# Attention planner: a table of parameters with finer rows, and the instruction orders that follow

## The chip, the cores and the metric

The kernel runs on one core of a Trainium2 chip. The metric is the device time of one execution in microseconds; lower is better. Five engines work from instruction queues of their own: PE (matrix multiply), ACT (activation functions), DVE (vector work), POOL (general elementwise work) and SP (which issues most DMAs).

## The reference

Two attention blocks over 2048 tokens of width 512, with 32 heads of 16, their outputs side by side:

```python
# A: linear attention
phi = lambda t: jnp.where(t > 0, t + 1, jnp.exp(t)) + 1e-6
pq, pk = phi(q), phi(k)
kv = jnp.einsum("bhsd,bhse->bhde", pk, v)
z = jnp.einsum("bhsd->bhd", pk)
num = jnp.einsum("bhqd,bhde->bhqe", pq, kv)
den = jnp.einsum("bhqd,bhd->bhq", pq, z)[..., None] + 1e-6
# B: softmax attention
scores = jnp.einsum("bhqd,bhkd->bhqk", q, k) * scale
p = _softmax(scores, axis=-1)
o = jnp.einsum("bhqk,bhkd->bhqd", p, v)
# both: q, k, v = x @ wqkv before, @ wo after; then
return jnp.concatenate([a, b], axis=-1)
```

The work is in B: 32 heads x 2048 x 2048 scores, each of which needs an exponential.

## The kernel before

**Work units.** B is cut into 32 units (NU): four groups of eight heads, four chunks of 512 queries, and two sets of four heads (even and odd). A unit has 64 score blocks (UB): 16 key tiles times four heads, each block 128 keys x 512 queries. So there are 2048 blocks. The four heads of a unit lie in the four row groups of PE's array, so up to four blocks are made at the same time.

**Two ways through a block.** PE makes the scores into a PSUM bank (`qk`, line 907). Then either

- ACT takes the exponential of two or three neighbouring banks in one instruction (`fill_act_cand`, line 1056; the instruction is line 1129), into as many slots of the shared buffer MEM. The planner calls the third block "more" (line 1082), and A3 in the table allows it. Banks 0, 1 and 4, 5 are ACT's pairs (SLOT); the third block takes bank 2 or 3 (OPT).
- or DVE computes an approximate exponential with integer arithmetic on the bits of an fp16 number (line 1008, one bank or two neighbouring ones), and POOL makes two shifted copies of the result (line 1204), so that this block fills three slots and is multiplied with three weighted versions of V. DVE's banks are 6, 3 and 2 (DSET).

PE then multiplies each slot with V into one PSUM bank (line 1259): one product for a block of ACT, three for a block of DVE. When a unit's products are complete, DVE transposes and normalizes them (lines 1289 to 1303).

**The rest of the work** is cut into jobs: projections of B (`proj_job`, `v4_job`; the matmuls in column tiles are line 644, the evacuations lines 681 to 751), the linear branch A (its exponentials are L768 on ACT, its other steps L769 to L829 on DVE), output projections (line 648 copies their results) and stores. They share PE, DVE and DVE's banks with B.

**The order.** The instruction order of each engine is found while the program is built, by a list planner (the loop from line 1527 on). It keeps a model clock T for each engine, collects what each could start next (`fill_act_cand`: scores for ACT; `fill_d_cand`: scores for DVE; `pv_cand`: products with V; `job_cand`: projections and the like), and takes the earliest, with priorities for ties. Thus nobody decides beforehand how many blocks go to DVE: it is what the order leaves. `fill_in` (line 1495) puts dummy matmuls (line 1518) into planned gaps of PE. Planned durations are in the code, for one exponential of ACT `d = 0.04 + w * 0.000845` us for w columns (line 1125), and for a change between PE's row, column and other tilings SW = 0.1 us.

**The table.** Thirteen parameters of the planner come from a table row, chosen by the model clock of PE:

```python
WAITN, WAITM, DLOW, DLOW2, PVO, PVQ, PVR, JPR, DLEAD, DBL, RES, LIM, A3 = TABLE[min(int(T["pe"] / TSEG), len(TABLE) - 1)]
```

- WAITN, WAITM, DLOW: when DVE's planned backlog is under DLOW, the next scores for ACT may be put off until WAITN of DVE's banks are free, so that scores for DVE go along with them.
- DLOW2: the backlog under which a third block for ACT is refused when DVE could have one. A3: whether a third block is allowed at all.
- PVO, PVQ, PVR: when a batch of products with V is taken, and how many rounds it may have.
- JPR: the priority of a job's matmuls. DLEAD, DBL: how early scores for DVE are made, and how large DVE's backlog may grow.
- RES: buffer slots kept in reserve. LIM: how close to ACT running dry other PE work may come.

The head of the program, up to the first exponential, is a hand-written order that the table doesn't touch. DMAs of the jobs are issued by SP in the order of the plan.

Of the kernel before, what the change touches and what calls it, by code (L numbers as in the profile page):

```python
# [259 lines left out]
def bass_concat_heads__linear_attn_block__softmax_full_mha__prompt_kernel(nc, A_x, A_wqkv, A_wo, B_x, B_wqkv, B_wo, out):  # L260
# [34 lines left out]
    TSEG = 5  # L295
    TABLE = [
        (2, 0.2, 0.3, 1, 8, 13.5, 2, 0.8, -0.5, 4, 6, 0.1, 1),
        (2, 0, 2, 0.6, 5, 10, 2, 0.8, 0.2, 4, 6, 0.15, 1),
        (2, 0, 2, 0.6, 5, 10, 2, 0.8, 0.2, 4, 6, 0.15, 1),
        (2, 0, 2, 0.6, 12, 11, 2, 0.8, 0.2, 4, 6, 0.15, 1),  # L300
        (2, 0, 1, 0.6, 12, 11, 2, 0.8, 0.5, 4, 6, 0.15, 1),
        (2, 0, 1, 0.6, 12, 11, 2, 0.8, 0.5, 2, 6, 0.15, 0),
        (2, 0, 1, 0.6, 12, 13.5, 2, 0.8, 0.5, 2, 8, 0.15, 0),
        (2, 0.1, 2, 0, 5, 12.5, 2, 2, -0.5, 3, 8, 0.15, 0),
        (1, 0.1, 0.6, 0, 5, 12.5, 2, 2, -0.5, 4, 8, 0.15, 0),
        (2, 0.1, 0.6, 0.6, 5, 12.5, 2, 2, -0.5, 4, 8, 0.15, 0),
        (2, 0, 1.5, 0.6, 12, 13.5, 2, 2, -0.5, 3, 8, 0.15, 0),
        (2, 0, 1.5, 0.6, 12, 13.5, 2, 0.8, -0.5, 3, 6, 0.15, 0),
        (1, 0, 1.5, 0.6, 5, 13.5, 2, 0.8, -0.5, 3, 4, 0.15, 0),
        (1, 0.1, 1.5, 0.6, 3, 13.5, 2, 2, -0.5, 3, 8, 0.15, 0),  # L310
        (1, 0, 0.6, 1, 16, 10, 2, 2, 0.5, 3, 4, 0.15, 0),
        (1, 0, 1, 1, 16, 8, 2, 2, 0.2, 3, 8, 0.15, 1),
        (1, 0, 1, 1, 3, 8, 2, 2, 0.2, 3, 6, 0.15, 1),
        (1, 0, 1, 0.3, 3, 8, 2, 0.8, 0.2, 3, 6, 0.1, 1),
        (3, 0, 2, 0.3, 3, 8, 2, 2, 0.2, 3, 6, 0.1, 1),
        (3, 0, 2, 0.3, 3, 8, 2, 2, 0.2, 2, 4, 0.15, 1),
        (3, 0, 2, 0.3, 16, 8, 2, 2, 0.2, 3, 4, 0.15, 1),
        (1, 0, 1.5, 0.3, 3, 11, 3, 2, -0.5, 2, 6, 0.06, 1),
        (1, 0, 1.5, 0.3, 3, 11, 2, 2, -0.5, 2, 6, 0.06, 1),
        (1, 0.1, 2, 0.3, 3, 11, 2, 2, 0, 2, 4, 0.15, 1),  # L320
        (1, 0, 2, 0.3, 3, 11, 2, 2, 0, 4, 4, 0.06, 1),
        (1, 0, 2, 0.3, 3, 12.5, 2, 2, 0, 4, 4, 0.1, 1),
        (1, 0, 2, 0.3, 3, 8, 3, 2, 0.5, 4, 4, 0.1, 1),
        (1, 0.2, 2, 0.3, 3, 8, 3, 2, 0.5, 2, 6, 0.1, 1),
        (1, 0.2, 2, 0.3, 3, 8, 3, 2, 0.5, 2, 6, 0.1, 1),
        (3, 0, 2, 0.3, 3, 8, 3, 2, 0.5, 2, 6, 0.1, 1),
        (2, 0.3, 1.5, 0, 16, 13.5, 2, 2, -0.5, 3, 6, 0.1, 1),
        (3, 0.3, 1.5, 0, 12, 13.5, 2, 2, 0.2, 3, 6, 0.1, 1),
        (2, 0.3, 1.5, 0.3, 3, 10, 2, 2, 0.2, 3, 6, 0.1, 1),
        (3, 0.3, 1.5, 0.3, 12, 13.5, 2, 0.8, 0.2, 3, 8, 0.1, 1),  # L330
        (3, 0.3, 1.5, 0.3, 12, 13.5, 2, 0.8, 0.2, 3, 8, 0.1, 1),
        (3, 0.05, 2, 0, 12, 13.5, 2, 0.8, 0, 3, 4, 0.1, 1),
        (3, 0.2, 1, 0, 5, 13.5, 2, 0.8, 0.8, 3, 6, 0.06, 1),
        (1, 0.1, 1.5, 0.6, 8, 13.5, 2, 0.8, 0.5, 4, 4, 0.06, 1),
        (3, 0.1, 1.5, 0.6, 8, 13.5, 2, 0.8, 0.5, 4, 4, 0.06, 1),
        (1, 0, 1, 0, 8, 8, 2, 2, -0.5, 4, 4, 0.15, 1),
        (1, 0, 1, 0, 8, 8, 2, 2, -0.5, 4, 4, 0.15, 1),
        (1, 0.1, 1, 1, 8, 12.5, 2, 2, -0.5, 2, 6, 0.15, 1),
        (1, 0.3, 2, 1, 8, 11, 2, 0.8, 0, 2, 6, 0.02, 0),
        (2, 0.05, 0.6, 0.3, 16, 8, 3, 0.8, 0.8, 4, 4, 0.06, 0),  # L340
        (1, 0.05, 1, 0.3, 5, 8, 2, 2, 0.2, 2, 6, 0.06, 1),
        (1, 0.2, 2, 0.3, 16, 8, 3, 2, -0.5, 2, 4, 0.06, 0),
        (1, 0.3, 2, 0.6, 12, 13.5, 3, 2, -0.5, 2, 4, 0.06, 0),
        (1, 0.3, 2, 0.6, 12, 13.5, 3, 2, -0.5, 2, 4, 0.06, 1),
        (1, 0.3, 2, 1, 16, 13.5, 2, 0.8, -0.5, 2, 4, 0.06, 1),
        (1, 0.1, 0.6, 0, 5, 9, 2, 2, 0, 2, 4, 0.06, 0),
        (1, 0.1, 0.3, 0, 5, 9, 2, 0.8, -0.5, 3, 8, 0.02, 0),
        (2, 0, 0.6, 0.3, 8, 13.5, 2, 2, -0.5, 2, 4, 0.06, 0),
        (2, 0.2, 0.3, 0.6, 12, 12.5, 2, 0.8, 0, 4, 8, 0.1, 0),
        (1, 0.1, 2, 0.6, 16, 12.5, 2, 0.8, 0.2, 3, 4, 0.15, 1),  # L350
        (1, 0.05, 2, 0.6, 16, 8, 2, 0.8, 0.2, 3, 8, 0.1, 1),
        (3, 0.05, 2, 0.6, 16, 8, 2, 0.8, 0.2, 4, 8, 0.02, 1),
        (3, 0.05, 0.6, 0.6, 16, 8, 2, 0.8, 0.5, 4, 8, 0.02, 1),
        (2, 0.05, 0.6, 0.6, 16, 8, 2, 0.8, 0.2, 4, 8, 0.02, 1),
        (2, 0.2, 2, 0.6, 8, 8, 3, 0.8, 0, 3, 8, 0.15, 1),
        (1, 0.1, 1.5, 0, 12, 13.5, 2, 0.8, -0.5, 2, 6, 0.02, 1),
        (1, 0.1, 1.5, 0, 12, 13.5, 2, 0.8, -0.5, 2, 6, 0.15, 1),
        (1, 0.1, 1, 1, 12, 13.5, 2, 0.8, -0.5, 2, 4, 0.15, 1),
        (1, 0.1, 1, 0, 12, 13.5, 2, 0.8, -0.5, 2, 4, 0.15, 1),
        (1, 0.1, 0.3, 0, 12, 13.5, 2, 0.8, -0.5, 4, 6, 0.15, 0),  # L360
        (1, 0.1, 2, 1, 12, 13.5, 2, 0.8, -0.5, 2, 8, 0.15, 1),
        (1, 0.1, 2, 1, 12, 13.5, 2, 0.8, -0.5, 2, 4, 0.15, 1),
        (1, 0.1, 2, 1, 12, 13.5, 2, 0.8, -0.5, 2, 4, 0.1, 1),
        (3, 0.2, 2, 0.6, 16, 12.5, 2, 0.8, 0.8, 3, 4, 0.15, 0),
        (3, 0.2, 2, 0.6, 16, 13.5, 2, 0.8, 0.8, 3, 4, 0.15, 0),
        (3, 0.2, 0.6, 0, 5, 13.5, 2, 0.8, 0.8, 3, 4, 0.1, 0),
        (3, 0.2, 0.6, 0, 12, 10, 2, 0.8, 0.8, 2, 4, 0.1, 0),
        (3, 0.3, 1, 0.6, 3, 8, 2, 0.8, 0.8, 2, 6, 0.15, 0),
        (2, 0.3, 1.5, 0.6, 3, 10, 2, 0.8, -0.5, 3, 6, 0.15, 1),
        (3, 0, 2, 0.6, 16, 9, 2, 0.8, 0.5, 4, 4, 0.15, 0),  # L370
        (2, 0.2, 1, 0.3, 5, 10, 2, 2, 0.2, 4, 6, 0.02, 0),
        (2, 0.2, 1, 0, 5, 8, 2, 2, 0.2, 4, 6, 0.02, 0),
        (1, 0.1, 2, 1, 12, 9, 2, 0.8, 0.5, 4, 4, 0.15, 0),
        (2, 0.1, 2, 1, 12, 9, 2, 0.8, 0.5, 4, 4, 0.15, 1),
        (1, 0.2, 1, 0.6, 16, 13.5, 2, 0.8, -0.5, 4, 4, 0.15, 1),
        (3, 0.1, 1, 0.6, 16, 9, 2, 0.8, -0.5, 4, 4, 0.15, 1),
        (1, 0.05, 2, 0.6, 12, 12.5, 2, 0.8, 0.2, 2, 4, 0.15, 1),
        (3, 0.1, 1.5, 0.6, 5, 9, 2, 0.8, 0, 3, 8, 0.15, 1),
        (1, 0.1, 1.5, 1, 16, 9, 2, 0.8, 0, 2, 8, 0.15, 1),
        (1, 0.1, 1.5, 0.6, 16, 9, 2, 0.8, 0.5, 2, 8, 0.15, 1),  # L380
        (1, 0.2, 1, 0.6, 5, 12.5, 2, 2, 0.5, 3, 8, 0.15, 1),
        (1, 0.2, 0.6, 0.6, 12, 10, 2, 2, 0, 2, 4, 0.1, 1),
        (3, 0, 1.5, 1, 5, 9, 2, 0.8, -0.5, 2, 6, 0.15, 1),
        (2, 0.2, 0.3, 0.6, 3, 9, 2, 2, 0, 2, 6, 0.06, 0),
        (1, 0.1, 2, 0.6, 5, 11, 2, 0.8, 0, 4, 8, 0.1, 1),
        (1, 0, 2, 0.6, 5, 11, 2, 0.8, 0, 4, 8, 0.1, 1),
        (1, 0.2, 2, 1, 5, 11, 2, 0.8, 0, 4, 4, 0.1, 1),
        (1, 0.2, 2, 0.3, 5, 11, 2, 0.8, 0, 4, 6, 0.1, 1),
        (1, 0.2, 1, 0.6, 5, 11, 3, 0.8, 0, 4, 4, 0.1, 1),
        (3, 0.3, 0.6, 1, 3, 9, 2, 0.8, -0.5, 2, 4, 0.06, 1),  # L390
        (1, 0.3, 0.6, 1, 5, 8, 2, 0.8, 0.5, 4, 4, 0.1, 1),
        (2, 0.3, 1.5, 1, 3, 8, 2, 0.8, -0.5, 2, 8, 0.06, 1),
        (2, 0.3, 1.5, 1, 5, 10, 2, 0.8, 0.2, 3, 8, 0.15, 1),
        (2, 0.2, 0.6, 0.3, 12, 8, 2, 0.8, 0.8, 4, 4, 0.15, 0),
        (3, 0, 0.6, 0.3, 8, 9, 2, 2, 0.5, 4, 6, 0.15, 0),
        (2, 0, 1, 0.3, 8, 10, 2, 0.8, 0.5, 4, 6, 0.15, 0),
        (1, 0.1, 0.3, 1, 3, 10, 2, 0.8, -0.5, 2, 8, 0.1, 0),
        (2, 0, 1, 0.3, 8, 10, 2, 0.8, 0.5, 4, 6, 0.15, 0),
        (2, 0, 1, 0.3, 12, 10, 2, 0.8, 0.2, 2, 6, 0.15, 0),
        (2, 0.1, 1, 0.3, 5, 9, 3, 0.8, 0, 2, 4, 0.15, 0),  # L400
        (1, 0, 0.6, 0, 8, 13.5, 3, 2, 0.8, 3, 4, 0.1, 0),
        (1, 0.1, 2, 0.6, 16, 8, 2, 2, 0, 3, 8, 0.02, 1),
        (2, 0, 2, 1, 5, 9, 2, 0.8, 0.5, 3, 8, 0.02, 1),
        (3, 0.05, 2, 0.3, 5, 12.5, 2, 2, 0.2, 4, 4, 0.1, 0),
        (3, 0.05, 2, 0.3, 5, 12.5, 2, 0.8, 0.5, 4, 8, 0.02, 0),
        (1, 0.05, 0.3, 1, 8, 10, 2, 0.8, -0.5, 4, 4, 0.02, 0),
        (1, 0, 0.3, 0.3, 8, 8, 2, 2, 0.5, 4, 4, 0.06, 1),
        (1, 0, 1, 0, 16, 9, 2, 0.8, 0, 3, 6, 0.15, 1),
        (2, 0.05, 2, 0.6, 3, 13.5, 2, 0.8, 0.8, 3, 8, 0.06, 1),
        (2, 0.05, 1.5, 1, 12, 10, 2, 2, 0.5, 2, 4, 0.06, 1),  # L410
        (1, 0.05, 2, 0.3, 5, 11, 2, 2, 0.8, 2, 8, 0.15, 1),
# [1278 lines left out]
```

## Time and profile before

| what | value |
|---|---|
| median of 3 runs (lowest, highest) | 656.95 us (656.53, 657.69) |
| the profiled execution, its own time | 655.85 us |
| its span, first to last instruction | 654.1 us |
| PE busy, instructions | 640.7 us (98%), 8388 |
| weight loads of PE (PEld) | 207.3 us (32%) |
| DVE | 594.7 us (91%), 1022 |
| ACT | 640.8 us (98%), 692 |
| POOL | 420.4 us (64%), 718 |
| mean granted TensorE clock | 0.997 |
| DMA | mean 27 GB/s over the span |

A row of the profile's groups names line, engine, operation, output and input tile and shape, the number of instructions, then their busy time and the mean time of one in ns, then the idle time of that engine just ahead of them and what ended it. The busy time is a union: instructions of one engine overlap in the record, so the mean of one is more than its share. In a row of busy times by stretch, the columns are the stretch, its length with the busy time of PE, then PEld, DVE, ACT and POOL, each with its number of instructions, then granted clock, DMA share and GB/s. A row of the timeline gives the start and length of a run of equal instructions.

### The profile page before, as it was taken

To read this page: it belongs to the slowest core of one execution; us is meant where nothing else is said; L and a number is where in the kernel's file an instruction comes from. 1 tells how busy PE (TensorE), PEld (TensorE's weight loads), DVE (VectorE), ACT (ScalarE), POOL (GpSimd) and SP (SyncE) were. 2 spreads that over 40 slices of the span, in tenths; PEclk is the share of its full clock that TensorE was granted. 3 is DMA by queue.
4 is the path that set the end of the run, shared out by engine and by line. 5 is a ranking of instruction groups with operands and counts; after the bars stand their busy time and mean duration, and the time that the engine had idled before them with its cause. 6 is when DMAs were issued, how large, how long until landed. Compare 5 with 4: busy or idle time off the path is not lost.

```text
span 654.1 us, 19881 instructions
## 1 busy us (share of the span) xinstructions
PE 640.7 (98%) x8388; PEld 207.3 (32%) x8389; DVE 594.7 (91%) x1022; ACT 640.8 (98%) x692; POOL 420.4 (64%) x718
## 2 busy tenths in 40 slices
PE   9999999999999999999999999999999999999996
PEld 5322333333443333333222222223332222222221
DVE  6999999978888989898999999999899999999994
ACT  6999999999999999999999999999999999999995
POOL 6588766634557656674667767766557756667772
PEclk9999999999999999999999999999999999999998
DMA  9910000000000000000011001100010100110011
GB/s 212 252 54 2 1 2 3 11 10 11 10 3 2 3 2 3 3 9 10 10 22 45 2 2 35 26 10 14 8 30 20 26 10 33 35 42 19 17 35 38
DMA packets 35808, 17.61 MB, mean 27 GB/s; under 512 B 26496, under 2 KB 35200, under 8 KB 35712
## 3 DMA queue, kind: packets, MB, share of 16 engines
q1 hardware_dynamic: 34512, 15.87, 10.0%
q8 instruction: 68, 1.11, 0.7%
q10 hardware_dynamic: 1200, 0.39, 0.2%
q14 instruction: 28, 0.23, 0.1%
HBM read 4.72 MB, written 4.19 MB: 14 GB/s over the span
## 4 chain that ended last, share of the span: by engine, by line
ACT 50%; PE 48%; issue 1%; DVE 1%; POOL 0%; DVEq 0%; ACTq 0%
ACT MEM L1129 48%; PE pS L907 17%; PE pPV L1259 17%; PE pS L644 8%; PE pS L746 2%; ACT EA L768 2%; PE pPV L1518 1%; PE pS L1367 1%; PE pS L794 1%; PE pS L1335 0%; PE pS L825 0%; PE pS L705 0%; PE pS L1390 0%; PE pS L1380 0%; DVE MEM L1008 0%
## 5 line engine op out<-in xcount | busy, mean ns | idle before, releaser
L1129 ACT ACTIVATE MEM<-pS 128x1024 f16<-128x1024 f32 (+1 forms) x653 | 632.1, 1298 | 0.5 <-PE pS L907 0.5
L1204 POOL INT64_ADD MEM<-MEM x691 | 412.7, 610 | 220.6 <-DVE MEM L1008 142.5
L1008 DVE TENSOR_SCALAR MEM<-pS 128x512 int16<-128x512 f32 (+1 forms) x654 | 440.7, 712 | 34.1 <-PE pS L907 31.1
L1259 PE MATMUL pPV<-MEM,VV 128*17 128x512 f16 x3426 | 272.3, 381 | 1.1 <-DVE OT L1289 0.8
L907 PE MATMUL pS<-QT,KM 32*128 32x512 bf16 x2048 | 258.1, 384 | 5.2 <-ACT MEM L1129 2.4
L907 PEld LDWEIGHTS pS<-QT,KM 32*128 32x128 bf16 x2048 | 66.1, 90 | 257.3 <-ACT MEM L1129 237.8
L1259 PEld LDWEIGHTS pPV<-MEM,VV 128*17 128x17 bf16 x3426 | 56.6, 88 | 107.2 <-issue 86.9
L644 PE MATMUL pS<-Wa,xTa 128*32 128x256 bf16 x1024 | 43.2, 275 | 0.1
L644 PE MATMUL pS<-MEM 128*32 128x512 bf16 x480 | 38.7, 384 | 0.1
L644 PEld LDWEIGHTS pS<-Wa,xTa 128*32 128x32 bf16 x1024 | 23.7, 96 | 13.4 <-issue 8.2
L768 ACT ACTIVATE EA<-pS 128x512 bf16<-128x512 f32 x32 | 26.3, 821 | 0.0
L1289 DVE STREAM_TRANSPOSE OT<-pPV 128x512 f32<-128x512 f32 x31 | 22.0, 708 | 1.9 <-PE pPV L1259 1.7
L644 PE MATMUL pS<-WOa,KNa 128*32 128x512 bf16 x256 | 21.3, 384 | 0.1
L648 DVE CAST KNa<-pS 128x512 bf16<-128x512 f32 x30 | 20.4, 682 | 1.0 <-PE pS L644 0.6
L746 PE MATMUL pS<-MEM 128*128 128x128 bf16 x256 | 20.0, 220 | 0.0
L644 PE MATMUL pS<-xTa,Wa 128*32 128x512 bf16 x256 | 19.5, 383 | 0.0
L746 PEld LDWEIGHTS pS<-MEM 128*128 128x128 bf16 x256 | 14.4, 98 | 8.2 <-issue 4.8
L644 PE MATMUL pS<-WOb,MEM 128*32 128x512 bf16 x192 | 15.5, 384 | 0.0
L644 PEld LDWEIGHTS pS<-MEM 128*32 128x32 bf16 x480 | 9.2, 94 | 14.3 <-issue 8.2
L1297 DVE TENSOR_TENSOR OT<-OT,ZR 128x256 bf16<-128x256 f32 x31 | 13.7, 442 | 0.0
L751 DVE CAST VV<-pS 128x512 bf16<-128x512 f32 x16 | 11.0, 685 | 1.1 <-PE pS L746 0.9
L787 DVE CAST VNa<-pS 128x512 bf16<-128x512 f32 x16 | 10.9, 684 | 0.8 <-PE pS L644 0.7
(84 smaller groups left out, 212.9 us busy)
## 6 DMA issues: line engine op xcount, KB each, us to landing
out_dram<-KNa SPq DMA_DIRECT2D x31, 128.0 KB, 1.7
Wa<-in_A_wqkv_dram SPq DMA_DIRECT2D x1, 1536.0 KB, 7.1
KM<-KR SPq DMA_DIRECT2D x96, 16.0 KB, 1.8
MEM<-in_B_wqkv_dram SPq DMA_DIRECT2D x2, 384.0 KB, 4.3
MEM<-in_B_x_dram SPq DMA_DIRECT2D x2, 256.0 KB, 3.5
MEM<-in_B_wqkv_dram SPq DMA_DIRECT2D x1, 512.0 KB, 4.5
WOb<-in_B_wo_dram SPq DMA_DIRECT2D x1, 512.0 KB, 8.0
WOa<-in_A_wo_dram SPq DMA_DIRECT2D x1, 512.0 KB, 10.3
```

Of the source, the lines that this page charges most:

```text
L644: ins = e.matmul(dst[32 * g:32 * g + 32, :], lhsT=lhsT[:, 32 * g:32 * g + 32], rhs=rhs, start=start, stop=stop, tile_position=(0, 32 * g))
L648: return lambda e, bk: (e.tensor_copy(out_fn(), in_fn(bk)) if lane == "dve" else e.activation(out_fn(), in_fn(bk), ACTF.Copy))
L746: return e.matmul(f32v(bk)[:, tl * 128:(tl + 1) * 128], lhsT=xTb[:, cc, t * 128:(t + 1) * 128], rhs=Wb[:, cc, 1024 + Gp * 128:1024 + Gp * ...
L751: st.append(("dve", 0.6, f_ev("dve", lambda e, bk: e.tensor_copy(VV[:, r, 0, 4 * t4:4 * t4 + 4, :].rearrange("p t (h c) -> p t h c", c=17) ...
L768: ("act", 0.06 + n * 0.000833, f_ev("act", lambda e, bk: e.activation(EA[:, q, 0:n], f32v(bk)[:, c0:c0 + n], ACTF.Exp), [], [("EA", q)])),
L907: return e.matmul(dst, lhsT=KM[32 * g:32 * g + 32, Gp % 2, e_, j * 128:(j + 1) * 128], rhs=QT[32 * g:32 * g + 32, Gp % 2, c * 512:(c + 1) ...
L1008: sch.add("dve", lambda e: e.tensor_scalar(PTi[:, i * 512:(i + n) * 512], PS[:, b0 * 512:(b0 + n) * 512], ESC, EB, op0=ALU.mult, op1=ALU.add),
L1129: sch.add("act", lambda e: e.activation(PT[:, p0 * 512:p0 * 512 + w], PS[:, use[0] * 512:use[0] * 512 + w], ACTF.Exp, scale=SC), reads=[(" ...
L1204: sch.add("pool", lambda e: e.int64_add(PTl[:, pos * 128:pos * 128 + w], PTl[:, p0 * 128:p0 * 128 + w], v_), extra_deps=port[0], reads=[(" ...
L1259: sch.add("pe", lambda e, g=g, j=j, hl=hl, pi=pi, k=k, first=first, last_=last_: e.matmul(PVb[32 * g:32 * g + 17, 0:512], lhsT=VV[:, Gp % ...
L1289: sch.add("dve", lambda e: e.transpose(OT[:, 0, :], PVb[:, 0:512]), reads=[("PV", g) for g in range(4)], writes=[("OT", 0)])
L1297: ("dve", _Port(0.355), f_op("dve", lambda e: e.tensor_tensor(xn[:, :, 16 * e_:16 * e_ + 16], o[:, :, 0:16], zr.unsqueeze(2).broadcast_to( ...
```

## The change

Only the planner's table is replaced, and with it the length of time that a row holds: 129 rows for 5 us each become 319 rows for 2 us each. At no whole microsecond of the model clock below 640 do the old and the new table give the same row; the row that both end in, in force from 640 us on, is the same. The old table's row changes 123 times on the way, the new one's 276 times. Over the first 654 us, A3 is 1 for 439 us in the old table and for 532 us in the new. Weighted by time, the mean of DLOW goes from 1.35 to 1.32, of DLOW2 from 0.52 to 0.57, of RES from 5.7 to 5.4, of JPR from 1.27 to 1.33; WAITN, PVQ and PVR stay nearly the same. No function, duration, tile or other constant of the planner is changed.

```diff
-    TSEG = 5
+    TSEG = 2
     TABLE = [
-        (2, 0.2, 0.3, 1, 8, 13.5, 2, 0.8, -0.5, 4, 6, 0.1, 1),
-        (2, 0, 2, 0.6, 5, 10, 2, 0.8, 0.2, 4, 6, 0.15, 1),
-        (2, 0, 2, 0.6, 5, 10, 2, 0.8, 0.2, 4, 6, 0.15, 1),
...
+        (2, 0, 1, 1, 12, 10, 2, 2, 0, 3, 4, 0.1, 1),
+        (2, 0, 1, 0.3, 12, 10, 2, 2, 0, 3, 8, 0.1, 1),
+        (2, 0, 1, 0.3, 12, 10, 2, 2, 0, 3, 8, 0.15, 1),
...
+        (1, 0.3, 1, 0, 12, 8, 3, 2, 0.2, 2, 4, 0.06, 1),
+        (3, 0.05, 0.6, 1, 6, 9, 2, 0.8, 0.5, 4, 4, 0.02, 1),
+        (3, 0.05, 0.6, 1, 6, 9, 2, 0.8, 0.5, 4, 4, 0.02, 1),
         (3, 0.05, 0.6, 1, 6, 9, 2, 0.8, 0.5, 4, 4, 0.02, 1),
     ]
```

## The prediction

> **What bounds the kernel now.** I read the page's groups first, then the groups kept apart by shape, then the timeline of one stretch, then the busy time in stretches of 50 us. The page's groups:
>
> ```profile
> L1129 ACT ACTIVATE MEM<-pS 128x1024 f16<-128x1024 f32 (+1 forms) x653 | 632.1, 1298 | 0.5 <-PE pS L907 0.5
> L1204 POOL INT64_ADD MEM<-MEM x691 | 412.7, 610 | 220.6 <-DVE MEM L1008 142.5
> L1008 DVE TENSOR_SCALAR MEM<-pS 128x512 int16<-128x512 f32 (+1 forms) x654 | 440.7, 712 | 34.1 <-PE pS L907 31.1
> L1259 PE MATMUL pPV<-MEM,VV 128*17 128x512 f16 x3426 | 272.3, 381 | 1.1 <-DVE OT L1289 0.8
> L907 PE MATMUL pS<-QT,KM 32*128 32x512 bf16 x2048 | 258.1, 384 | 5.2 <-ACT MEM L1129 2.4
> ```
>
> The column to read is the idle time ahead of the group. ACT's 653 exponentials waited 0.5 us in all; DVE's exponentials waited 34.1 us, nearly all for PE's scores; POOL waited 220.6 us. ACT is the bound, and it is not "98%" full but full without a gap from its first exponential to its last (the 13.3 us that it is idle lie at head and tail). The same groups by shape:
>
> ```profile
> L1129 ACT ACTIVATE MEM<-pS 128x1024 f16<-128x1024 f32 x600 | 576.9, 1265 | 0.5 <-PE pS L907 0.5
> L1008 DVE TENSOR_SCALAR MEM<-pS 128x512 int16<-128x512 f32 x619 | 400.4, 683 | 32.3 <-PE pS L907 29.4
> L1129 ACT ACTIVATE MEM<-pS 128x1536 f16<-128x1536 f32 x53 | 88.6, 1673 | 0.0
> L1008 DVE TENSOR_SCALAR MEM<-pS 128x1024 int16<-128x1024 f32 x35 | 42.7, 1219 | 1.8 <-PE pS L907 1.7
> L768 ACT ACTIVATE EA<-pS 128x512 bf16<-128x512 f32 x32 | 26.3, 821 | 0.0
> ```
>
> They split the 2048 score blocks (the x2048 of L907): ACT takes 600 x 2 + 53 x 3 = 1359, DVE 619 + 35 x 2 = 689. A DVE block is multiplied with V three times: 1359 + 3 x 689 = 3426, the count of L1259, so the split is right. A recorded mean of 1265 ns is not the price, since one instruction is recorded from before its predecessor ends. The price is the cadence:
>
> ```profile
> 379.74 0.40 PE L907 MATMUL pS<-QT,KM 32*128 32x512 bf16 x4
> 380.07 0.61 PE L1259 MATMUL pPV<-MEM,VV 128*17 128x512 f16 x8
> 380.66 0.39 PE L907 MATMUL pS<-QT,KM 32*128 32x512 bf16 x3
> 380.98 0.61 PE L1259 MATMUL pPV<-MEM,VV 128*17 128x512 f16 x8
> 381.58 0.39 PE L907 MATMUL pS<-QT,KM 32*128 32x512 bf16 x4
> 381.90 0.61 PE L1259 MATMUL pPV<-MEM,VV 128*17 128x512 f16 x7
> 382.49 0.39 PE L907 MATMUL pS<-QT,KM 32*128 32x512 bf16 x3
> ```
>
> PE makes scores each time ACT hands back two banks: 379.74, 380.66, 381.58, 382.49, which is 2.75 / 3 = 0.917 us for one two-block exponential. The end times of ACT in the trace say the same: 0.917 us for two blocks, 1.344 for three, 0.490 for the L768 ones. The difference, 0.427 us, is one more block; so an instruction costs 0.063 us and a block 0.427. The sum: 600 x 0.917 + 53 x 1.344 + 32 x 0.490 = 637.1 us. ACT's last evacuation ahead of the stream ends at 7.68, its last exponential at 645.14 (timeline): 637.5. The span is 7.7 head + 637.5 of ACT + 9.0 tail = 654.1; around it lie 1.75 us (655.85 for this execution), and the median of the runs is 1.1 above that.
>
> So the change pays only by what leaves ACT: **one block moved to DVE is worth 0.917 / 2 = 0.458 us**; a three-block exponential in place of one and a half of two saves half an instruction, 0.0315 us.
>
> **The change, part by part.** Constants, engines, tiles and operations stay. Head (written by hand up to 7.7 us) and the last table row (equal in both) stay, so head and tail are costed at nothing, within 0.5 us for the tail. The linear branch's L768 and all projections stay in number, moved in time only. Their DMAs move too, on SP's queue; in the list of waits down to 0.5 us, no compute engine waits for a DMA, so nothing, while a job that must wait for a landing (1.7 to 2.5 us) is planned behind other work. No wait is added by hand; where order puts a PV batch ahead of scores, ACT is who waits.
>
> *What else a moved block costs.* DVE: six in a row take 3.82 us (timeline, 382.58), (3.82 - 0.68) / 5 = 0.63; with pairs in one instruction 1.22 / 2 = 0.61. I take 0.61. POOL: two shifted copies, 691 instructions of 0.61 us for 1378 copies, so 0.61 us, against 220 us idle: hidden; without that cover 0.61 us of PV delay, not ACT time. PE: two more PV products, eight per 0.43 us, so 0.11; a score group costs 0.32 us to the next PV and one goes per two blocks (-0.16 per block) when the block rides as third or fourth of another group. PE's cost lies between -0.05 and +0.11 us.
>
> *How many blocks can move.* Busy time in stretches (time, then PE, PEld, DVE, ACT, POOL):
>
> ```profile
> 60.00:110.00 50.00, 49.30 (x727) 16.28 (x723) 47.50 (x84) 50.00 (x57) 36.43 (x62) 1.00 0.01 2
> 110.00:160.00 50.00, 49.86 (x791) 19.18 (x787) 42.29 (x76) 50.00 (x52) 23.79 (x41) 1.00 0.04 10
> 160.00:210.00 50.00, 49.62 (x679) 19.69 (x679) 43.95 (x78) 50.00 (x52) 30.44 (x51) 1.00 0.02 4
> 510.00:560.00 50.00, 49.14 (x611) 13.73 (x611) 48.36 (x86) 50.00 (x58) 32.62 (x55) 1.00 0.08 22
> 560.00:610.00 50.00, 49.89 (x618) 12.57 (x610) 47.98 (x80) 50.00 (x54) 35.21 (x60) 1.00 0.14 36
> ```
>
> DVE is idle 44.2 us between 10 and 640, unevenly: 7.7 us at 110:160, 6.1 at 160:210, but 2.0 at 560:610. Moving d blocks takes 0.61 d of it, and the span shrinks by 0.458 d: all of it is gone at d = 44.2 / 1.07 = 41, a gain of 19 us. That is the outer end. The inner end is zero or below: DVE's idle time is time without scores, and order may not bring them sooner. Between them the nearest row is the kernel's own middle stretch. The twelve full stretches have a median of 2.85 us idle; if the six above it (7.7, 6.1, 3.2, 5.4, 3.5, 4.0, together 29.9) came down to it, 12.8 us would be won, d = 12. I take two thirds, d = 8, since 110:210 also carries the linear branch's K and V and the next group's projections, which must stand somewhere. **8 x 0.458 = 3.7 us.** The 16 further PV products cost PE 0.9 us at most, and four fewer score groups give back 1.3.
>
> *Three-block exponentials.* A3 is 1 during 439 of 654 us in the old table, 532 in the new. In proportion, 53 become 64: 11 x 0.0315 = **0.35 us**.
>
> Sum: 3.7 + 0.35 = 4.0 us; 656.95 - 4.0 = 652.9 (in a profiled execution 655.85 - 4.0 = 651.8).
>
> *A rule against the row.* The Trainium skill, Perfetto Trace Analysis, section "Identifying the Most-Contended Engine", says that matmul busy time is a poor measure of the tensor engine's closeness to its limit, and that its weight-load share is a better one. By it PE at 98% is a false alarm: PEld is 32%, so PE would never hold d back, d could go to 41 and the time to 638. The row says otherwise here: from scores to PV is 0.32 us, from PV to scores 0.59, and 0.32 + 0.59 is ACT's whole 0.91 us, of which only 0.22 + 0.43 is columns flowing; the rest is the gap at each switch of row tiling, which weight-load share doesn't count. PE's order is thus a limit of its own, and I hold to the row. The same page ("Optimizing Scalar/DVE Operations") warns that GpSimd and DVE share an SBUF port, so that work moved between them may not pay. A moved block adds POOL work, but it is POOL that waits here (17.1 us for L769, 14.9 for L1297, out of 220); those DVE instructions waited 2.4 and 0.0. By the rule the 8 blocks' POOL time could come off DVE, 4.9 us or 5 blocks of gain; by the row nothing. I take the row.
>
> **Rivals.**
> *A plan that improves on paper only* (no change). The planner reckons 0.04 + 1024 x 0.000845 = 0.905 us per two-block exponential; the chip takes 0.917. Over 653 instructions ACT runs 7.8 us behind the plan, so up to that much of planned ACT gaps is invisible on the chip. If the search closed such gaps and left 689 blocks with DVE, the time is 656.9. For it: ACT has no gap now. Against it: 0.458 us per block is also the planner's largest lever.
> *A large gain.* Every stretch as full as 560:610 (2.0 idle per 50): 44.2 - 25.2 = 19 us, d = 18, 8.2 us: 648.4, with A3's part. Against it: PE at 110:260 has hardly a dummy matmul (L1518) to give up.
> *Slower: three-block exponentials starve DVE.* The third block takes bank 2 or 3, two of DVE's three banks (6, 3, 2). By shape, 60:110 has no three-block exponential and 61 DVE blocks, 110:160 has 12 and 40: up to 1.75 blocks lost for each. But 160:210 has 9 and 50, 210:260 none and 53: 0.33 each. It decides from 0.0315 / 0.458 = 0.07 block lost for each, without a gain in order elsewhere. The place: 210:260 and 310:360, where A3 rises from 0.3 and 0.4 of the time to 0.8. At one block each, 11 x (0.458 - 0.0315) = 4.7 us slower: 661.6. Against it: the rows also raise DLOW2, under whose backlog the third block is refused when DVE could have one.
>
> **How the numbers follow.** A measurement of this kernel can tell 0.2% from no change, which is 1.3 us or three blocks. Gain of 3 to 13 blocks (651 to 655.6): 0.64. More than 13: 0.14. On paper only: 0.14. Slower: 0.08. Range: up to 657.3, leaving out the slower case and a quarter of the unchanged one (0.12), and down to 649.0, 17 blocks with A3's share, leaving out a third of the large gain (0.05).
>
> **What would show it.** L1008 should stand for about 697 blocks (instructions plus the two-block ones once more), L1259 for 3442, L1129 for 1351; three-block exponentials near 64; ACT's idle ahead of L1129 still under 1 us; DVE's idle at 110:210 below 13.8. Wrong: L1259 at 3426 or fewer with the time down or ACT gaps of microseconds; or a head or tail that moved by over 0.5 us.

## The result, and the profile after

The changed kernel takes 652.34 us (median of four runs, 652.05 to 652.82), against 656.74 for the kernel before beside it: 4.4 us less, ratio 0.9932, 95% interval 0.9915 to 0.995. The prediction was 652.9. The profiled execution took 652.82 us, with a span of 651.1. The groups by shape of the changed kernel; all lines below the table have moved down by 190, so L1319 is the old L1129, L1198 the old L1008, L1449 the old L1259:

```profile
L1319 ACT ACTIVATE MEM<-pS 128x1024 f16<-128x1024 f32 x580 | 561.1, 1252 | 1.1 <-PE pS L1097 1.1
L1198 DVE TENSOR_SCALAR MEM<-pS 128x512 int16<-128x512 f32 x627 | 405.9, 684 | 30.3 <-PE pS L1097 26.4
L1449 PE MATMUL pPV<-MEM,VV 128*17 128x512 f16 x3446 | 275.7, 383 | 1.2 <-DVE OT L1479 1.0
L1319 ACT ACTIVATE MEM<-pS 128x1536 f16<-128x1536 f32 x63 | 103.0, 1653 | 0.4 <-PE pS L1097 0.4
L1198 DVE TENSOR_SCALAR MEM<-pS 128x1024 int16<-128x1024 f32 x36 | 44.0, 1222 | 1.9 <-PE pS L1097 1.8
```

ACT has 580 x 2 + 63 x 3 = 1349 blocks, DVE 627 + 36 x 2 = 699, and 1349 + 3 x 699 = 3446 is the count of L1449. So ten blocks have moved from ACT to DVE, and ten more exponentials take a third block. At the cadences of before, which still hold (0.917, 1.344 and 0.490 us from end to end in this trace too), ACT's work is 580 x 0.917 + 63 x 1.344 + 32 x 0.490 = 632.2 us, 4.9 less than 637.1.

The span fell by 3.0 only, and the idle column says why: 1.5 us ahead of ACT's exponentials, where there was 0.5. The rows of ACT's timeline at that place, and PE's clock in the stretches around it (the first number after the five pairs):

```profile
529.20 5.95 ACT L1319 ACTIVATE MEM<-pS 128x1024 f16<-128x1024 f32 x6
535.54 1.45 ACT L1319 ACTIVATE MEM<-pS 128x1536 f16<-128x1536 f32 x1 [0.38 <-PE pS L1097]
537.61 7.93 ACT L1319 ACTIVATE MEM<-pS 128x1024 f16<-128x1024 f32 x8 [0.61 <-PE pS L1097]
```

```profile
530.00:535.00 5.00, 4.38 (x56) 1.52 (x55) 4.74 (x11) 5.00 (x6) 2.43 (x5) 0.86 0.00 0
535.00:540.00 5.00, 5.00 (x62) 1.36 (x59) 3.67 (x6) 4.00 (x5) 2.40 (x4) 0.80 0.01 3
540.00:545.00 5.00, 5.00 (x71) 1.35 (x62) 5.00 (x8) 5.00 (x6) 3.92 (x7) 1.00 0.08 26
```

The granted clock fell to half for 3.4 us (one record of the trace, 3413 ns long), and scores came late: two exponentials ended 1.2 us behind their cadence here. Over the whole stream ACT lost, by its end times, 1.6 us against the next profile of this kernel. The ledger of the profiled pair: head 0.3 shorter, ACT's stream 3.2 shorter (4.9 of work less 1.6 of gap), tail 0.5 longer: 3.0.

DVE between 10 and 640 us is idle 39.1 us, 44.2 before. Five of its stretches:

```profile
60.00:110.00 50.00, 48.86 (x743) 16.70 (x744) 48.10 (x80) 50.00 (x57) 37.11 (x63) 1.00 0.01 2
110.00:160.00 50.00, 49.81 (x753) 17.84 (x745) 43.83 (x79) 50.00 (x53) 27.68 (x47) 1.00 0.04 10
160.00:210.00 50.00, 49.94 (x716) 21.18 (x712) 42.73 (x81) 50.00 (x51) 27.28 (x46) 1.00 0.02 5
510.00:560.00 50.00, 49.25 (x614) 13.71 (x606) 47.07 (x81) 49.00 (x55) 32.41 (x55) 0.97 0.06 18
560.00:610.00 50.00, 49.64 (x614) 13.16 (x606) 49.55 (x82) 50.00 (x55) 38.32 (x64) 1.00 0.12 33
```

The two stretches that were emptiest, 110 to 210, are as empty as before together (13.4 against 13.8 us); the one at 560, already among the fullest, has 0.45 us idle where it had 2.0.

### The profile page after: what moved, and what is told of

Read it like the earlier page. It is cut to its first block, busy times and chain, and to the rows that moved or that the text cites. A ratio compares the mean times of both kernels' runs of the same rounds, so it can differ in the third digit from the quotient of the medians.

```text
span 651.1 us, 19936 instructions
## 1 busy us (share of the span) xinstructions
PE 636.3 (98%) x8402; PEld 207.0 (32%) x8403; DVE 599.1 (92%) x1031; ACT 636.6 (98%) x682; POOL 427.2 (66%) x729
## 4 chain that ended last, share of the span: by engine, by line
PE 52%; ACT 45%; DVE 1%; DMA 1%; issue 0%; POOL 0%; SPq 0%; DVEq 0%
ACT MEM L1319 44%; PE pPV L1449 19%; PE pS L1097 18%; PE pS L834 9%; PE pS L936 2%; ACT EA L958 2%; PE pS L895 1%; DMA MEM<-in_B_x_dram 1%; PE pPV L1708 0%; PE pS L1525 0%; PE pS L984 0%; PE pS L905 0%; DVE MEM L1198 0%; PE pS L1580 0%; DVE KNa L838 0%
## 5 line engine op out<-in xcount | busy, mean ns | idle before, releaser
L1319 ACT ACTIVATE MEM<-pS 128x1024 f16<-128x1024 f32 (+1 forms) x643 | 628.2, 1291 | 1.5 <-PE pS L1097 1.5
L1394 POOL INT64_ADD MEM<-MEM x702 | 419.5, 611 | 210.5 <-DVE MEM L1198 132.4
L1198 DVE TENSOR_SCALAR MEM<-pS 128x512 int16<-128x512 f32 (+1 forms) x663 | 446.7, 713 | 32.3 <-PE pS L1097 28.3
L1449 PE MATMUL pPV<-MEM,VV 128*17 128x512 f16 x3446 | 275.7, 383 | 1.2 <-DVE OT L1479 1.0
L1449 PEld LDWEIGHTS pPV<-MEM,VV 128*17 128x17 bf16 x3446 | 57.1, 88 | 109.2 <-issue 89.1
L1487 DVE TENSOR_TENSOR OT<-OT,ZR 128x256 bf16<-128x256 f32 x31 | 13.8, 446 | 0.0
```

Of the source, the lines that this page charges most:

```text
L1198: sch.add("dve", lambda e: e.tensor_scalar(PTi[:, i * 512:(i + n) * 512], PS[:, b0 * 512:(b0 + n) * 512], ESC, EB, op0=ALU.mult, op1=ALU.add),
L1319: sch.add("act", lambda e: e.activation(PT[:, p0 * 512:p0 * 512 + w], PS[:, use[0] * 512:use[0] * 512 + w], ACTF.Exp, scale=SC), reads=[(" ...
L1394: sch.add("pool", lambda e: e.int64_add(PTl[:, pos * 128:pos * 128 + w], PTl[:, p0 * 128:p0 * 128 + w], v_), extra_deps=port[0], reads=[(" ...
L1449: sch.add("pe", lambda e, g=g, j=j, hl=hl, pi=pi, k=k, first=first, last_=last_: e.matmul(PVb[32 * g:32 * g + 17, 0:512], lhsT=VV[:, Gp % ...
L1487: ("dve", _Port(0.355), f_op("dve", lambda e: e.tensor_tensor(xn[:, :, 16 * e_:16 * e_ + 16], o[:, :, 0:16], zr.unsqueeze(2).broadcast_to( ...
```

## The experiments

The theory under test: **the time is head + ACT's instructions at their cadence (0.063 us each and 0.427 per block) + tail**, so the order is worth what it takes from ACT. Its rival: PE and DVE bind as much (the chain of the changed kernel goes through PE for 52% of the span), and ACT's fullness is a result of their pace. Differences are against the changed kernel's median of 651.9 or its span of 650.2, from its second profile, unless another is named. The experiments ran on several chips, and the kernel before, run beside each, took 656.4 to 657.1 us, so a few tenths between experiments mean nothing. The head of that second profile is 8.5 us long, where the others have 7.4 to 8.3; so the length of ACT's stream, from its last evacuation in the head to its last exponential (632.6 us there), is the cleaner measure, and stands beside the span.

**The changed kernel again.** 

> The changed kernel once more, for a second profile. Theory (the time is head + ACT's instructions at their cadence + tail): 580 x 0.917 + 63 x 1.344 + 32 x 0.490 = 632.2 us of ACT without the 1.3 us gap that the first profile shows at 535 to 541, so a span near 650 and a profiled time near 651.8, if the dip of the granted clock in that gap is a matter of one execution. Rival (the gap belongs to the new order): the gap is there again and the span is 651.

Measured: 651.9 us (651.63 to 653.36), before beside it 657.08, ratio 0.9927 (0.991 to 0.9943). The profile's span is 650.2, with no dip before the tail:

```profile
L1319 ACT ACTIVATE MEM<-pS 128x1024 f16<-128x1024 f32 x580 | 561.0, 1253 | 0.5 <-PE pS L1097 0.5
L1319 ACT ACTIVATE MEM<-pS 128x1536 f16<-128x1536 f32 x63 | 103.5, 1660 | 0.0
```

The gap is gone with the dip, and the sum of ACT's steps from end to end is 632.6 us. The dip belongs to an execution, not to every run of the order. The span without it is 3.9 below before: ACT's stream is 4.9 shorter, as counted (632.6 against 637.5), the head 0.8 and the tail 0.2 longer.

**More work for ACT.**

```diff
+                    extra[0] += 1
+                    if extra[0] % 31 == 0:
+                        for _ in range(2):
+                          sch.add("act", lambda e: e.activation(DY[:], ZW[:], ACTF.Exp), reads=["ZW"], writes=["DY"])
```

> The changed kernel with 40 more exponentials on ACT (128x256 from SBUF, result unused), two after every 31st exponential of scores. Estimated at 0.063 + 0.427 / 2 = 0.28 us each: 11 us. Theory (ACT is full and nothing else binds): the whole 11 us, 663. Rival (PE and DVE bind as much, ACT's fullness is a result of their pace): well under half, 652 to 657.

Measured: 667.2 us, 15.3 more; span 664.2, 14.0 more, ACT's stream 14.5 more. Of the four runs, two at a mean clock of 0.999 took 666.0 (14.1 more), two at 0.993 and 0.994 took 668.4.

```profile
L1321 ACT ACTIVATE MEM<-pS 128x1024 f16<-128x1024 f32 x580 | 555.2, 1169 | 0.5 <-PE pS L1099 0.5
L1326 ACT ACTIVATE DY<-ZW 128x256 bf16<-128x256 bf16 x40 | 21.1, 526 | 0.6
```

The estimate for one was too low: by ACT's end times the 40 took 14.9 us, 0.37 each (0.295 for the first of a pair, 0.449 for the second; why the second costs more stays open). So nearly the whole of it is in the time, as the theory says, while its price per instruction and block, taken from exponentials that read PSUM, does not carry over to these.

**More work for DVE.**

```diff
+                    extra[0] += 1
+                    if extra[0] % 32 == 0:
+                        sch.add("dve", lambda e: e.tensor_reduce(DY[:, 0:2], ZW[:].unsqueeze(1).broadcast_to([128, 2, 256]), axis=AX.X, op=ALU.max), reads=["ZW"], writes=["DY"])
```

> The changed kernel with 20 more instructions on DVE (a maximum over 512 columns from SBUF, about 0.6 us each as other 512-column ones, 12 us in all, result unused), one after every 32nd approximate exponential. Theory: DVE has some 40 us of idle time and its banks are made ahead; 0 to 3 us, 652 to 655. Rival (DVE is a bound too, and the gain came from filling it): 8 to 12 us, 660 to 664.

Measured: 655.76 us (median of 17 runs), 3.9 more; span 653.6, 3.4 more, and ACT's stream 3.4 more. The 20 took 0.592 us each by DVE's end times, 11.8 in all, so a third was paid, in delays of 0.1 to 0.3 us at some fifteen of ACT's exponentials. A third lies between the two expectations, nearer the theory's: DVE's idle time is slack, but not free.

**More work for PE.**

```diff
+                extra[0] += 1
+                gz = [g for g in range(4) if pv_iss[u][g] > 0 and pv_rem[u][g] > 0]
+                if extra[0] >= 21 and gz:
+                    extra[0] = 0
+                    def more(e, g=gz[0]):
+                        for i in range(6):
+                            ins = e.matmul(PVb[32 * g:32 * g + 17, 0:256], lhsT=ZW[:, 0:17], rhs=ZW[:], start=False, stop=False, tile_position=(0, 32 * g))
+                        return ins
+                    sch.add("pe", more, reads=["ZW"], writes=[("PV", gz[0])], accum=("pv", u, gz[0]))
```

> The changed kernel with 23 groups of 6 dummy matmuls on PE (256 columns of zeros added into the bank of products with V, 0.107 us each, 14.8 us in all), spread evenly. Theory (ACT bounds, PE is a limit of its own for how many blocks can move, but it has slack between two exponentials): each 0.64 us group eats a slack of some 0.4 us, so 2 to 7 us, 654 to 659. Rival (PE is the bound, as the chain's 52% says): 13 to 15 us, 665 to 667.

Measured: 660.85 us, 9.0 more of the 14.8 added; the span of its profile is 660.3, with a half-clock dip at about 542 us that costs 1.4 of it (ACT's stream is 10.6 longer, so 9.2 without the dip). The rows of ACT in that profile:

```profile
L1320 ACT ACTIVATE MEM<-pS 128x1024 f16<-128x1024 f32 x580 | 555.4, 1143 | 7.0 <-PE pS L1098 6.7
L1320 ACT ACTIVATE MEM<-pS 128x1536 f16<-128x1536 f32 x63 | 97.7, 1565 | 0.5 <-PE pS L1098 0.4
```

Now ACT waits for scores. Both expectations miss: three fifths were paid, more than the theory's 2 to 7 us and less than the rival's 13 to 15. A group of 0.64 us cost 0.39 on average, so PE's slack between two exponentials is nearer 0.25 us than the 0.4 I had taken. ACT is the bound of this order, PE stands close behind, and DVE farther off. The added work came in lumps of some 0.6 us on both; whether the same work in smaller pieces would have been hidden was not tried.

**One parameter alone.**

Only the last place of a row differs, at 195 of 640 us (on for 51 of them where it was off, off for 144 where it was on); at 24 us it is the first time:

```diff
-        (1, 0.1, 2, 1, 8, 13.5, 2, 2, 0.5, 3, 4, 0.15, 0),
+        (1, 0.1, 2, 1, 8, 13.5, 2, 2, 0.5, 3, 4, 0.15, 1),
...
```

> The new table with one of its thirteen parameters, A3, set at each time to what the old table has there; all else as in the changed kernel. The planner then gives DVE 622 blocks instead of 699, and 104 three-block exponentials instead of 63. Theory (the time is ACT's instructions at their cadence: 0.063 us each plus 0.427 per block, and single parameters have no worth of their own): ACT 1426 x 0.427 + 661 x 0.063 = 650.5 against 616.6 us, so 33.9 more than the changed kernel: 686. Rival (as the prediction had it, a parameter acts by itself: A3 is worth the three-block exponentials that it allows): within 2 us of the changed kernel, 650 to 654.

Measured: 688.2 us, 36 more; the formula without gaps says 34, and ACT's end times show 2.7 us of gaps over the changed kernel's. From the profile (by shape, first lines for ACT and DVE):

```profile
L1660 ACT ACTIVATE MEM<-pS 128x1024 f16<-128x1024 f32 x557 | 543.1, 1229 | 2.4 <-PE pS L1438 2.4
L1539 DVE TENSOR_SCALAR MEM<-pS 128x512 int16<-128x512 f32 x578 | 376.1, 683 | 61.9 <-PE pS L1438 58.2
L1660 ACT ACTIVATE MEM<-pS 128x1536 f16<-128x1536 f32 x104 | 163.2, 1631 | 0.0
```

DVE's wait for scores doubles, 77 blocks go back to ACT. So the values of A3 have no worth of their own: one parameter out of thirteen, set to values that serve in the other table, costs eight times what the change gained. (The other twelve were not exchanged singly.) With A3 on for less of the time, there are more three-block exponentials, not fewer. They stand where DVE takes few blocks: from 310 to 360 us, 12 of them with 29 blocks on DVE, against 7 with 57 in the changed kernel. Whether DVE fell behind first and left banks free for a third block, or third blocks took the banks that DVE needed, this run does not tell.

**Rows of both tables.**

The first row that differs from the new table is that of 450 us:

```diff
-        (1, 0.05, 2, 0, 8, 11, 2, 2, 0, 2, 8, 0.1, 1),
+        (1, 0.2, 2, 1, 5, 11, 2, 0.8, 0, 4, 4, 0.1, 1),
...
```

> The new table's rows until 450 us of the model clock, the old table's rows after that. Stretch by stretch the new table is ahead before 450 and DVE takes 682 blocks in all, fewer than under either whole table (689 and 699). Theory (a row fits only the state that its own predecessors leave; time by ACT's count): 1366 x 0.427 + 649 x 0.063 = 624.2 against 616.6 us, 7.6 more than the changed kernel: 660, slower than before. Rival (rows are good or bad for their stretch): between before and changed, 652 to 656.

Measured: 660.2 us, 8.3 more than the changed kernel and 3.5 more than before (ratio 1.0051, 1.0028 to 1.0074); 604 + 39 x 2 = 682 blocks on DVE. The rows from 450 on belong to a kernel with 689 blocks, follow rows of a kernel with 699, and give fewer than either: by the traces DVE has begun 491 blocks at 460 us (old table 484, new 491), and takes 191 after that (old 205, new 208). That speaks against rows which are good or bad for their stretch whatever came before, and fits the theory, in this one mix.

**The three-block exponential.**

```diff
+                    for lo, hi in ([(0, 2), (2, 3)] if n == 3 else [(0, n)]):
-                        sch.add("act", ... PT[:, p0 * 512:p0 * 512 + w], PS[:, use[0] * 512:use[0] * 512 + w] ...)
+                        sch.add("act", ... PT[:, (p0 + lo) * 512:(p0 + hi) * 512], PS[:, (use[0] + lo) * 512:(use[0] + hi) * 512] ...)
```

> The changed kernel, each of its 63 three-block exponentials issued as one of two blocks and one of one block; order, blocks per engine and all other instructions as they were. Theory (0.063 us per ACT instruction and ACT full): 63 x 0.063 = 4.0 us more, span 654.2 against 650.2, time 656. That is the whole of the change's gain lost by a cost that the prediction put at 0.0315 us per three-block exponential where it takes the place of one and a half two-block ones. Rival (the larger part of an instruction's cost is hidden behind the one before, as the records overlap): under 1.5 us, 652 to 653.5.

Measured: 655.96 us (median of 20 runs), 4.1 more; span 654.0, 3.8 more; ACT's stream 636.6, 4.0 more. Against the kernel before beside it, 656.67, only 0.7 us of the gain is left.

```profile
L1320 ACT ACTIVATE MEM<-pS 128x1024 f16<-128x1024 f32 x643 | 623.6, 1270 | 0.5 <-PE pS L1097 0.5
L1320 ACT ACTIVATE MEM<-pS 128x512 f16<-128x512 f32 x63 | 52.5, 834 | 0.0
```

The one-block parts end 0.490 us after their predecessor, the two-block ones 0.917. The instruction's 0.063 us is all in the time, though the records of two instructions overlap by far more than that (834 ns recorded for a one-block part, 490 paid).

**More dummy matmuls.**

```diff
-            low = sum(y - max(x, st - 3.2) for x, y in hot) < 0.5 * 3.2
+            low = sum(y - max(x, st - 3.2) for x, y in hot) < 0.7 * 3.2
```

> The changed kernel with more dummy matmuls in the gaps that the plan has anyway (a gap is filled whole when PE was under 70% busy in the 3.2 us before, not under 50%): 106 instead of 65. The plan and every other instruction stay. In the changed kernel the granted clock fell to half for 3.4 us at 534 us in the first profile, and the ACT gap of 1.3 us stands there; in the second profile neither. Theory (the dip is set off by the low activity of PE at 531 to 534, and fires in some executions only): no dip at 534 in any execution, so single times between 651.5 and 652.3, without the ones at 652.8 and 653.4 of the changed kernel; the median 0.1 to 0.4 lower. Rival (the dip is not a matter of activity, or the added matmuls get in the way of scores): some executions again over 652.7, or a median above 652.3.

Measured: 652.03 us, five runs from 651.69 to 652.64, mean clock 0.997 to 0.999 in each. The changed kernel was run 13 times in all: four of its executions have a mean clock of 0.996, and take 652.8 to 653.4 us; the other nine take 651.3 to 652.5. So what these four share costs some 1.1 us on average (one of them was profiled, and shows the dip), and none of it fell into these five. Five without a dip would come by chance in one case out of six at that rate, and the median is lower by less than the spread; one of the five, 652.64, lies above the 652.3 that the theory allowed. Not settled. The activity of PE around 534 us is low in each profile of this order, and dips in the profiles of two others of its kin (with PE's extra work, and the order with other rows from 528 us on, below) fall at this place too. But low activity by PE's busy time does not decide alone. In the 3.41 us just before the dip of the first profile, from 530.22 on, PE is busy for 2.79 us. In the profile of the changed kernel that stands beside the next experiment the same stretch, 529.93 to 533.35, has 2.81, and no dip follows; with ACT's extra work, 355.91 to 359.33 has 2.56, and none follows either.

**Against the planner's own clock.**

```diff
-        (2, 0, 1.5, 1, 12, 11, 2, 0.8, 0.5, 2, 4, 0.15, 1),
-        (2, 0, 1.5, 1, 12, 11, 2, 0.8, 0.5, 4, 4, 0.1, 1),
+        (2, 0, 1.5, 1, 12, 12.5, 2, 0.8, 0.5, 3, 4, 0.1, 1),
+        (2, 0, 1.5, 1, 12, 12.5, 2, 0.8, 0.5, 3, 4, 0.1, 1),
...
```

> The changed kernel once more, to stand beside the next kernel on the same chip: 652.3, with a spread of 1.5 us upwards from the executions in which the clock dips.

> The new table with other rows from 528 us on, found by a search of mine over those rows. By the planner's own clock this order ends 0.3 us later than the changed kernel (638.09 against 637.77), as it leaves ACT 1.4 us more of planned gaps; but DVE takes 701 blocks, not 699 (ACT: 582 exponentials of two blocks, 61 of three). Theory (time goes by ACT's count, and planned gaps of ACT are hidden since the chip's ACT runs 0.012 us per exponential behind the plan): 0.85 us less of ACT, 651.5 if nothing else, faster than both kernels. Rival (time goes by the planner's end): 0.3 us more, 652.6; or the gaps show, 652.9.

Measured: the changed kernel beside it 652.2 us (651.3 to 653.02), this one 652.58 (651.66 to 652.78): no gain, and no loss that stands out of the spread. ACT did get its 0.9 us less (the sum of its steps is 633.0 us with 1.3 in a dip, against 632.6), but in this pair of profiles the tail took it. The rows of ACT after its last exponential, first in this kernel, then in the changed one beside it:

```profile
627.21 13.20 ACT L1320 ACTIVATE MEM<-pS 128x1024 f16<-128x1024 f32 x13
643.99 0.60 ACT L839 ACTIVATE KNa<-pS 128x512 bf16<-128x512 f32 x1 [3.58 <-PE pS L1526]
645.28 0.60 ACT L839 ACTIVATE KNa<-pS 128x512 bf16<-128x512 f32 x1 [0.70 <-PE pS L1526]
```

```profile
626.78 13.20 ACT L1319 ACTIVATE MEM<-pS 128x1024 f16<-128x1024 f32 x13
642.88 1.08 ACT L838 ACTIVATE KNa<-pS 128x512 bf16<-128x512 f32 x2 [2.90 <-PE pS L1525]
```

The stream ends at 627.21 + 13.20 = 640.4 and the program at 651.0, 10.6 later; in the other it is 640.0 and 649.6, 9.6. The output projections of the last tile wait 0.7 us longer, and their copies stand apart. What is longer is what PE still owes when ACT is done: its last products with V, 52 in a row, run from 638.49 to 641.68, 1.3 us past ACT's stream; in the changed kernel the last two end at 640.58, 0.6 past it. The planned gaps of ACT were hidden, as my theory had it; what PE then owes it had not counted. Head + ACT + tail holds, but the tail is not a constant when blocks are moved late. No version here beat the changed kernel.

## Why the prediction was right

*ACT as the bound, 0.458 us per block.* Held over a wide range. With 689, 682 and 622 blocks on DVE the count of ACT's instructions and blocks puts the time 4.9, 7.6 and 33.9 us above the changed kernel's; the chip showed 4.4, 8.3 and 36.3. In the profiles ACT's stream fell by 4.9 us, from 637.5 to 632.6, as counted. ACT's added work came through nearly whole.

*d = 8 blocks.* It was 10, and this is the term that was short, by 0.9 us. Its derivation did not hold as written, so that 8 came near 10 is in part luck. I took the gain from the six stretches with over 2.85 us idle and called 110:210 their chief reserve; in the second profile those six gave 4.2 us of 29.9, the other six 3.4 of 12.6, and the last 30 us lost 1.8. The sum, 5.8 us, is 10 blocks at nearly 0.6, and so is the growth of the approximate exponentials' own busy time, from 440.7 to 446.7 us in the first profile. So the price of 0.61 was about right and the place was not: the gain is spread, and the stretch with the most idle time, 110:210, kept nearly all of it (13.4 of 13.8 us in the first profile, 13.0 in the second).

*Three-block exponentials: 11, 0.35 us.* There are 10, but the inference from A3's share of the time has nothing in it, as the exchange of A3 alone shows (104 where the share fell). Right by chance. Their worth, 0.0315 us each, is shown by splitting them.

*The sum.* 4.0 us foretold; ACT's work shrank by 4.9, and the medians show 4.4 (4.3 and 5.2 in two more comparisons, 656.49 and 657.08 against 652.2 and 651.9). The medians scatter by about as much as the sum missed.

*Head and tail.* Costed at nothing, with over 0.5 us named as a sign of being wrong. In the three profiles of the changed kernel the head is 7.4, 8.5 and 7.4 us, the tail 9.5, 9.2 and 9.6, where one profile of before has 7.7 and 9.0. So one program's head moves by 1.1 us from one execution to another, and the sign was set too tight; whether the tail's 0.2 to 0.6 belong to the new order, one profile of before can't tell.

*The other signs.* Blocks on DVE were 699 for 697, products with V 3446 for 3442, ACT's blocks 1349 for 1351. ACT's idle time ahead of its exponentials, foretold under 1 us, was 1.5 with the dip and 0.5 without.

*PE as a limit of its own.* The row was the better guide than the weight-load share: 14.8 us of matmuls more cost 9.0, so PE was no engine with two thirds free. The page cited, Perfetto Trace Analysis of the Trainium skill, section "Identifying the Most-Contended Engine", asks for the kernel's share of the peak FLOPs beside the weight-load share, which the prediction left out and no run here works out. What the weight-load share misses shows in the trace of before: two rounds of products in the same tiling start 0.22 us apart (380.07 and 380.29), scores and the products that follow 0.32. My own figure for its slack was too kind all the same. DVE's idle time was not free either: a third of added DVE work was paid, and the outer end of 41 blocks, reckoned from idle time alone, is farther off than it looked.

*The shared port.* Ten more blocks gave POOL 11 more instructions. A one-bank exponential of DVE took 684 ns against 683, POOL's copies 611 against 610. So nothing came off DVE's price, as the row had it; no run here sets out to test the port.

*The rivals.* On paper only: no, as blocks did move. Starved DVE: the changed order has none of it at 210:260 and 310:360, where A3 rose (3 and 7 three-block exponentials where there were 0 and 2, with 54 and 57 blocks on DVE where there were 53 and 57). What a real mismatch of rows does is the 36 us above, and starved DVE may have its part in that. That it is so large a matter I had not foreseen: the slower case was priced at 4.7 us.

*What stays open.* The runs show why ten blocks fewer on ACT are worth the time, not which rows gave the ten. How much of the gain is the choice of values and how much the finer rows can't be told from these two tables. And what sets off the dip of the clock, and whether more dummies would keep it up for good.

## What to carry to other kernels

Where one engine has no gap, count its instructions at their end-to-end cadence: the change of that count is the forecast, and idle time elsewhere only bounds it. Take the cadence from instructions of the same kind. Values found for a whole order are best treated as one object: here neither reading A3 by itself nor mixing the two tables worked. Test how near the second engine stands by adding work to it; busy shares said 98% for both ACT and PE here, and of the work added (14.9, 14.8 and 11.8 us) ACT paid nearly all, PE three fifths, DVE a third.

## What was not expected of the hardware

The TensorE clock fell to half in the middle of a stream of matmuls in which, at 530 to 535 us, records still show PE busy for 4.38 of 5 us, and came back after 3413 ns. The second profile of the same program has 4.39 of 5 there and no dip. The records of the granted clock in the first profile are 529.066 us at full clock, 3.413 at half and 112.640 at full, which is 155, 1 and 33 times 3.4133: the clock changed in steps of that length, counted from 4.57 us. In the second profile they count from 6.92, so the steps lie differently over the same order; whether that is why one execution dips and another does not, the profiles don't tell. By their mean clock and time four of 13 executions of one program had it (only one of the four was profiled), at about 1.1 us each, a quarter of what the change gained. So one program can have two levels of time 0.2% apart; the spread of single times shows it before the median does.
